# Attention and MLP on one TensorE stream: a slot's attention work at 14 points instead of 7

## The chip, the cores and the metric

The kernel runs on one core of one Trainium2 chip. The metric is the device time of one execution in microseconds (us).

## The reference

The reference is an attention block with normed queries and keys, followed by a two-layer MLP without biases. Inputs are float32; the two MLP weights come as float64.

```python
# q, k, v: (8 batches, 12 heads, 448 positions, 64)
q_n, k_n = (rmsnorm(q, g_q), rmsnorm(k, g_k))     # x / sqrt(mean(x*x) + 1e-6) * g
scores = (1 / 8) * q_n @ k_n.T                    # softmax over keys follows
attn_out = softmax(scores) @ v
x = attn_out.transpose(0, 2, 1, 3).reshape(3584, 768)
h = x @ w_in                                      # 768 x 2048
out = (h - tanh(h)) @ w_out                       # 2048 x 768
```

## The kernel before

The attention of one batch and two heads is a step; there are 8 x 6 = 48 steps, and the work around a step is a slot. The MLP is a Python generator that emits one matmul at a time, batch after batch. A slot emits its attention work by hand and calls `run(ns)` between pieces of it; `run` takes matmuls from the generator until their nominal time has been reached. [...]

**The MLP's stream.** From the second batch on each layer is done by seven products for every set of blocks instead of eight (Strassen's scheme in Winograd's form, order 1, 5, 6, 2, 3, 7, 4). A batch's hidden layer has 4 sets of 7 products of 6 matmuls (168 in all), its output layer 3 sets of 7 products of 8 matmuls (168). Every matmul has 224 columns. `product` (L738) emits the matmuls (L750), then the follow-up that earlier products left in `late["todo"]`, then `use`, which reads the product's PSUM bank. These follow-ups are: copies of product 1 on ACT (L804, L867), sums on DVE (L806 for product 5, L808 for 6, L812 and L813 for 7, L816 for 3, L820 for 4; L869 to L881 in the output layer), tanh on ACT and the subtraction on DVE for product 2 (L786, L787), the same on POOL for the others (L787), the factors of the next layer (L797, L798 on DVE, L799 and L831 on POOL), and the output's transpose (L845 on DVE). Three PSUM banks serve the products. Products 2, 3 and 7 accumulate in the bank of products 1, 5 and 6 and so wait until that has been read. Weights come through a ring of six slots that SP fills five products ahead (L397, L399).

**The slots from the second batch's MLP on** (`slot`, s from 12 to 47). A slot begins with the visit: the scores of step s+1 for the last chunk of keys (L521), then the values of step s mixed with the other scores of step s+1, the exponentials on ACT (L527), and the division (L687 on ACT, L688 and L692 on DVE). Then follow 56 matmuls of the stream, in eight calls of `run` of 7 matmuls each; between them stand pieces of work for later steps. In slot s they are:

- for step s+1: the sum of the exponentials over chunks of keys (`add`, L552 and L553; `add_last`, L560); `fold` turns it on DVE (L657) and reduces it (L659); `gather` copies the parts together on ACT (L667); `spread_sums` reduces, inverts and widens (L675, L676, L678) and turns back (L680).
- for step s+2, from step 15 on by blocks of 32: `square_blocks` (ACT, L466), `norm_blocks` (reduce L473, four copies L475, L476 and L477 on DVE, and the power -1/2 on POOL, L478), `scale_blocks` (DVE, L485), `turn_blocks` for q (DVE transpose L495) and for k (DVE transpose L499, then ACT's multiplication by the gains, L500). Step 14 is still turned by TensorE (`turn`).
- loads on SP: v of step s+2 and q, k of step s+3 (L462) at the head of the stream part; in slot 12 alone the q, k of step 15 stand late in it.

So kT of step s+2, made in slot s, is read by the first matmul of slot s+1. A batch's MLP fills six slots: three hidden slots (s mod 6 = 0, 1, 2), then three output slots. In a hidden slot the products end after these counts of the slot's matmuls: first 6, 12, ... 54; second 4, 10, ... 52; third 2, 8, ... 56. In an output slot they end at 8, 16, ... 56.

Of the kernel before, what the change touches and what calls it, by code (L numbers as in the profile page):

```python
# [9 lines left out]
F32 = mybir.dt.float32  # L10
# [3 lines left out]
ALU = mybir.AluOpType  # L14
# [130 lines left out]
def bounded_path(tc, ctx, q, k, v, moe_w_in, moe_w_out, out, g_col, ident, ones, half_ones, neg_half, early):  # L145
# [17 lines left out]
    nc = tc.nc  # L163
# [17 lines left out]
    BL = 32  # L181
# [33 lines left out]
    def load(s, names):  # L215
        b, hp = steps[s]
        for name in names:
            src = {"q": q, "k": k, "v": v}[name]
            if s == 0 and name != "v":
                t = early[name]  # L220
            else:
                shape = [CP, 2, NCH, D] if name == "q" else [P, NCH, 2, D] if name == "k" else [P, 2, NCH, D]
                t = nat.tile(shape, F32, name=f"{name}_nat", bufs=3 if name == "v" else 2)
                fetch(nc, name, t, src[b, 2 * hp : 2 * hp + 2], in_order(s))
            loaded[name, s] = t
# [176 lines left out]
    normed, turned, probs, sums, whole, xT, tt = {}, {}, {}, {}, {}, {}, {}  # L402

    def squares(s):
        squares_of(nc, early["sq"], early["n"], loaded["q", s], loaded["k", s])

    def norm(s):
        rr = normed[s] = small.tile([P, 2, 2 * NCH], F32, name="rr", bufs=3) if s else early["rr"]
        if s:
            norm_of(nc, rr, early["sq"], early["n"], neg_half)  # L410
# [16 lines left out]
    def turn(s, tk, tq):  # L427

        rr, n = normed.pop(s), early["n"]
        kn = loaded.pop(("k", s))  # L430
        for c in range(NCH):
            nc.tensor.transpose(tk[:, c * P : (c + 1) * P], kn[:, c].rearrange("p h d -> p (h d)"), ident)
        kT = qkp.tile([P, S], F32, name="kT")
        nc.scalar.mul(kT, tk[:, :S], g_col)
        for c in range(NCH):
            nc.tensor.transpose(
                tq[:, c * CP : (c + 1) * CP], n[:, c].rearrange("p h d -> p (h d)"), ident[:CP, :CP]
            )
        qT = qkp.tile([P, S], F32, name="qT")
        nc.scalar.copy(out=qT, in_=tq[:, :S])  # L440
        turned[s] = rr, kT, qT
# [3 lines left out]
    FIRST, NJ = 2, S // BL  # L445
    TURNED = 2 * NP + 3

    def by_blocks(s):
        return has(s) and s >= TURNED
# [14 lines left out]
    def square_blocks(s):  # L464
        sq = normed[s] = late["blocks"].tile([P, 2, NJ, BL], F32, name="qk_n", bufs=1)
        nc.scalar.activation(  # L466
            sq.rearrange("p i j d -> p (i j d)"), loaded["qk", s].rearrange("p i j d -> p (i j d)"), AF.Square
        )

    def norm_blocks(s):  # L470

        mine, other = (late["blocks"].tile([P, 2 * NJ], F32, name=name, bufs=2) for name in ("rr_mine", "rr_other"))
        nc.vector.reduce_sum(mine, normed[s].rearrange("p i j d -> p (i j) d"), axis=AX.X)  # L473
        for g in range(P // BL):
            nc.vector.tensor_copy(out=other[g * BL : (g + 1) * BL], in_=mine[(g ^ 1) * BL : ((g ^ 1) + 1) * BL])  # L475
        nc.vector.tensor_tensor(out=mine, in0=mine, in1=other, op=ALU.add)  # L476
        nc.vector.tensor_scalar(out=mine, in0=mine, scalar1=1.0 / D, scalar2=1e-6, op0=ALU.mult, op1=ALU.add)  # L477
        nc.gpsimd.tensor_tensor(  # L478
            out=mine, in0=mine, in1=neg_half[:, :1].to_broadcast([P, 2 * NJ]), op=ALU.pow
        )  # L480
        normed["rr", s] = mine

    def scale_blocks(s):
        n, rr = normed[s], normed.pop(("rr", s))
        nc.vector.tensor_tensor(  # L485
            out=n.rearrange("p i j d -> p (i j) d"), in0=loaded.pop(("qk", s)).rearrange("p i j d -> p (i j) d"),
            in1=rr[:, :, None].to_broadcast([P, 2 * NJ, BL]), op=ALU.mult,
        )
# [15 lines left out]
    def sc_bank():  # L504
        return bank_of("sc")
# [34 lines left out]
    def full(s):  # L540

        return probs[s, 0][:, :, 0], probs[s, 1][:, :, 1], probs[s, 2][:, :, 0]

    def add(s):

        if s <= NP + NP // 2:
            sums[s] = []
            return
        t = early["sum"]
        sums[s] = [t]  # L550
        p = full(s)
        nc.vector.tensor_tensor(out=t, in0=p[0], in1=p[1], op=ALU.add)  # L552
        nc.vector.tensor_tensor(out=t, in0=t, in1=p[2], op=ALU.add)  # L553

    def add_last(s):
        last = probs[s, KF][:, :, 0]
        for n in range(2 if sums[s] else 0):
            t = sums[s][0]
            part = t[n * KR : (n + 1) * KR, :, n * HS : (n + 1) * HS]
            nc.vector.tensor_tensor(out=part, in0=part, in1=last[n * KR : (n + 1) * KR], op=ALU.add)  # L560
# [90 lines left out]
    FOLDED = 2 * NP + 1  # L651

    def fold(s):

        t = sums.pop(s)[0].rearrange("p h s -> p (h s)")
        turned_sum = late["blocks"].tile([P, 2 * S], F32, name="sum_T")
        nc.vector.transpose(out=turned_sum, in_=t)  # L657
        part = late["blocks"].tile([P, 2 * NJ], F32, name="sum_32")
        nc.vector.reduce_sum(part, turned_sum.rearrange("p (i k) -> p i k", k=BL), axis=AX.X)  # L659
        acc = whole[s] = late["blocks"].tile([2 * BL, P // BL, NJ], F32, name="sum_g")  # L660
        whole["part", s] = part

    def gather(s, h):

        acc, part = whole[s], whole["part", s]
        for g in range(P // BL):
            nc.scalar.copy(  # L667
                out=acc[h * BL : (h + 1) * BL, g], in_=part[g * BL : (g + 1) * BL, h * NJ : (h + 1) * NJ]
            )

    def spread_sums(s):

        acc = whole[s]
        total = late["blocks"].tile([2 * BL, NJ], F32, name="sum_all")
        nc.vector.reduce_sum(total, acc.rearrange("p g j -> p j g"), axis=AX.X)  # L675
        nc.vector.reciprocal(total, total)  # L676
        wide = late["blocks"].tile([2 * BL, NJ, BL], F32, name="sum_w")
        nc.vector.tensor_copy(out=wide, in_=total[:, :, None].to_broadcast([2 * BL, NJ, BL]))  # L678
        rs = whole[s] = late["blocks"].tile([2 * BL, S], F32, name="rs_T")
        nc.vector.transpose(out=rs, in_=wide.rearrange("p j k -> p (j k)"))  # L680

# [33 lines left out]
    late = {}  # L715
# [223 lines left out]
    def run(ns):  # L939

        spent[1] += ns
        while spent[0] + 1.0 < spent[1]:
            took = next(stream, None)
            if took is None:
                return
            spent[0] += took
# [10 lines left out]
    def has(s):  # L957
        return 0 <= s < NS
# [69 lines left out]
    def slot(s):  # L1028

        gap = gap_ns(s)  # L1030
        av = av_banks
        if has(s + 1):
            scores(s + 1, KF)
        if s < FOLDED:
            last_values(s, av)
            totals(s, sc_bank())
            divide(s, values(s, av))
            for c in range(KF):
                scores(s + 1, c)
        else:  # L1040
            visit(s, av)
        if has(s + 2):
            load(s + 2, "v")
        if by_blocks(s + 3) and s + 3 > TURNED:
            load_blocks(s + 3)
        blocks = by_blocks(s + 2)
        run(gap / 2)
        if has(s + 1):
            add(s + 1)
        if blocks:  # L1050
            square_blocks(s + 2)
        run(gap / 2)
        if blocks:
            norm_blocks(s + 2)
        elif has(s + 2):
            turn(s + 2, sc_bank(), sc_bank())
        ahead = has(s + 3) and not by_blocks(s + 3)
        if ahead:
            squares(s + 3)
        if has(s + 4) and not by_blocks(s + 4):  # L1060
            load(s + 4, "qk")
        run(gap / 2)
        folded = has(s + 1) and s + 1 >= FOLDED
        if has(s + 1):
            add_last(s + 1)
        if folded:
            fold(s + 1)
        run(gap / 2)
        if blocks:
            scale_blocks(s + 2)  # L1070
        if ahead:
            norm(s + 3)
        if folded:
            gather(s + 1, 0)
        run(gap / 2)
        if blocks:
            turn_blocks(s + 2, 0)
        if folded:
            gather(s + 1, 1)
        run(gap / 2)  # L1080
        if blocks:
            turn_blocks(s + 2, 1)
        if s + 3 == TURNED:
            load_blocks(s + 3)
        if ahead:
            norm_q(s + 3)
        run(gap / 2)
        if folded:
            spread_sums(s + 1)
        run(gap / 2)  # L1090

    load(0, "qk")
    load(1, "qk")
# [355 lines left out]
```

## Time and profile before

| | |
|---|---|
| median of 3 runs | 1391.6 us (1391.22 to 1391.68) |
| the profiled execution's own time | 1391.42 us |
| its span in the profile | 1389.6 us |
| TensorE busy | 1354.1 us (97% of the span) |
| VectorE (DVE) busy | 941.0 us (68%) |
| ScalarE (ACT) busy | 504.7 us (36%) |
| GpSimd (POOL) busy | 561.8 us (40%) |
| granted TensorE clock | 0.992 |
| L478, the power | 33 times, 4.8 us each |
| DVE's L485 waiting for L478 | 15.4 us in 21 waits |
| PE's L750 waiting for L806 | 4.2 us in 7 waits |

Times in a timeline count from the span's start. A line gives start, duration, engine, code line, operation, output<-input and, in brackets, how long the engine was idle before it and what released it. PE is the matmul, PEld the load of its weights, which can overlap it. SPq and the like are an engine's issuing queue. The ends of matmuls are modelled, so stalls of TensorE are best read from the starts.

### The profile page before, as it was taken

How to read it: one execution, taken by the hardware profiler on the slowest of the kernel's cores; microseconds unless marked ns; L12 is line 12 of the kernel's file. 1: busy time of each engine (PE TensorE's matmuls, PEld its weight loads, DVE VectorE, ACT ScalarE, POOL GpSimd, SP SyncE). 2: the span in 40 equal slices, each digit the busy share in tenths (PEclk: the TensorE clock that was granted, in tenths of full speed). 3: DMA queues.
4: the chain of work that ended last, by engine and by line, in shares of the span. 5: the costliest groups of instructions: out<-in, count | busy, mean ns of one | idle time of the engine just before them, and what ended most of it. 6: DMA issues, size and time to landing. Idle time of an engine off the chain costs nothing.

```text
span 1389.6 us, 29917 instructions
## 1 busy us (share of the span) xinstructions
PE 1354.1 (97%) x11840; PEld 1128.4 (81%) x11840; DVE 941.0 (68%) x1545; ACT 504.7 (36%) x1147; POOL 561.8 (40%) x345
## 2 busy tenths in 40 slices
PE   7989899999999999999999999999999999999997
PEld 3458654478898898899889988988988998899997
DVE  4899888856876788567866668657875677633311
ACT  7856554234322433324332343324333234301100
POOL 4656565223642356225444236323552354402310
PEclk9999999999999999999999999999999999999999
DMA  7888778766666666666657666666567667366663
GB/s 170 187 218 240 249 232 222 206 181 170 177 181 160 177 172 165 176 170 181 178 152 195 177 156 188 172 162 183 165 167 176 181 173 189 100 189 184 191 194 90
DMA packets 367657, 249.91 MB, mean 180 GB/s; under 512 B 281748, under 2 KB 309780, under 8 KB 367508
## 3 DMA queue, kind: packets, MB, share of 16 engines
q1 hardware_dynamic: 367504, 247.90, 66.5%
q8 instruction: 96, 1.57, 0.5%
q14 instruction: 53, 0.43, 0.1%
q10 hardware_dynamic: 4, 0.00, 0.0%
HBM read 214.40 MB, written 33.42 MB: 178 GB/s over the span
## 4 chain that ended last, share of the span: by engine, by line
PE 85%; DMA 6%; DVE 4%; SPq 2%; ACT 1%; issue 1%; POOL 1%; ACTq 0%; DVEq 0%; POOLq 0%
PE mm L750 65%; PE sc L521 8%; PE sc L582 6%; PE mm L915 4%; DMA w_raw<-in_moe_w_in_dram 2%; DMA w_f<-w_out 1%; PE sc L570 1%; DMA gT<-in_moe_w_in_dram 1%; DMA w_raw<-in_moe_w_out_dram 1%; DMA k_nat<-in_k_dram 1%; SPq L272 1%; DVE w_out L82 1%; DVE w_out L79 1%; PE sc L620 1%; DVE w_out L335 0%
## 5 line engine op out<-in xcount | busy, mean ns | idle before, releaser
L750 PE MATMUL mm<-xT,w_f 128*128 128x224 f32 x1392 | 278.5, 354 | 1.7 <-DVE s L806 1.7
L750 PEld LDWEIGHTS mm<-xT,w_f 128*128 128x128 f32 x1392 | 261.3, 190 | 16.0 <-issue 10.2
L750 PEld LDWEIGHTS mm<-gT,w_f 128*128 128x128 f32 x1344 | 252.8, 190 | 12.8 <-issue 12.8
L750 PE MATMUL mm<-gT,w_f 128*128 128x224 f32 x1344 | 263.0, 354 | 0.0
L478 POOL TENSOR_TENSOR rr_mine<-rr_mine,neg_half 128x28 f32<-128x28 f32 x33 | 159.7, 4839 | 218.2 <-DVE rr_mine L477 218.2
L521 PE MATMUL sc<-qT,kT 64*32 64x448 f32 (+1 forms) x3072 | 217.4, 503 | 10.0 <-ACT p_last L527 9.0
L750 PE MATMUL mm<-tt,w_f 128*128 128x224 f32 x1044 | 208.7, 353 | 0.0
L750 PEld LDWEIGHTS mm<-tt,w_f 128*128 128x128 f32 x1044 | 197.0, 190 | 4.4 <-issue 4.4
L787 POOL TENSOR_TENSOR gT<-s,th 128x448 f32<-128x448 f32 x96 | 120.4, 1262 | 197.0 <-ACT th L786 188.2
L750 PE MATMUL mm<-tg,w_f 128*128 128x224 f32 x1008 | 197.5, 352 | 0.0
L750 PEld LDWEIGHTS mm<-tg,w_f 128*128 128x128 f32 x1008 | 190.7, 190 | 0.0
L521 PEld LDWEIGHTS sc<-qT,kT 64*32 64x32 f32 x3072 | 71.1, 107 | 78.5 <-issue 56.2
L688 DVE TENSOR_TENSOR xT<-xT,sc 128x448 f32<-128x448 f32 x35 | 21.7, 621 | 166.5 <-PE sc L521 110.8
L710 POOL TENSOR_TENSOR tt<-xT,tt 128x224 f32<-128x224 f32 x23 | 31.1, 1353 | 234.2 <-DVE xT L692 212.0
L667 ACT COPY sum_g<-sum 32x14 f32<-32x14 f32 x280 | 56.3, 201 | 186.2 <-DVE sum L659 180.5
L582 PE MATMUL sc<-p,v_nat 64*32 64x448 f32 x1120 | 110.5, 536 | 0.0
L786 ACT ACTIVATE th<-s 128x448 f32<-128x448 f32 x96 | 55.2, 575 | 112.7 <-DVE s L812 59.8
L527 ACT ACTIVATE p<-sc 128x448 f32<-128x448 f32 x132 | 71.7, 543 | 51.7 <-PE sc L521 39.1
L915 PE MATMUL mm<-gT,w_out 128*128 128x448 f32 x192 | 75.9, 551 | 0.2 <-POOL w_out L90 0.2
L915 PEld LDWEIGHTS mm<-gT,w_out 128*128 128x128 f32 x192 | 36.3, 193 | 38.3 <-issue 35.8
L582 PEld LDWEIGHTS sc<-p,v_nat 64*32 64x32 f32 x1120 | 40.6, 107 | 31.0 <-issue 31.0
L142 POOL TENSOR_TENSOR rr<-rr,neg_half 112x8 f32<-112x8 f32 (+1 forms) x30 | 49.0, 1660 | 33.7 <-DVE rr L141 33.6
(151 smaller groups left out, 1828.3 us busy)
## 6 DMA issues: line engine op xcount, KB each, us to landing
w_f<-w_in SPq DMA_DIRECT2D x196, 384.0 KB, 3.3
w_f<-w_out SPq DMA_DIRECT2D x147, 512.0 KB, 4.2
w_raw<-in_moe_w_out_dram SPq DMA_DIRECT2D x16, 768.0 KB, 5.2
out_dram<-th SPq DMA_DIRECT2D x192, 56.0 KB, 1.9
w_in<-w_out SPq DMA_DIRECT2D x21, 384.0 KB, 5.9
qk_nat<-in_q_dram SPq DMA_DIRECT2D x132, 56.0 KB, 2.5
qk_nat<-in_k_dram SPq DMA_DIRECT2D x132, 56.0 KB, 2.6
v_nat<-in_v_dram SPq DMA_DIRECT2D x72, 96.0 KB, 3.7
```

The source lines that it names most:

```text
L142: nc.gpsimd.tensor_tensor(out=r, in0=r, in1=neg_half[:rows], op=ALU.pow)
L478: nc.gpsimd.tensor_tensor(out=mine, in0=mine, in1=neg_half[:, :1].to_broadcast([P, 2 * NJ]), op=ALU.pow)
L521: nc.tensor.matmul(tiles[h][i * BL : (i + 1) * BL, :n], lhsT=kT[r, c * P + at : c * P + at + BL], rhs=qT[r, first : first + n], start=True ...
L527: nc.scalar.activation(p[:, h, c if c < 2 else 0, :], tiles[h][:, :n], AF.Exp, scale=1.0 if rr is None else rr[:, 0, 2 * c + h : 2 * c + h ...
L582: nc.tensor.matmul(av[g][i * BL : (i + 1) * BL, :S], lhsT=v_nat[keys, h, c, m * BL : (m + 1) * BL], rhs=p[keys, h], start=first, stop=True ...
L667: nc.scalar.copy(out=acc[h * BL : (h + 1) * BL, g], in_=part[g * BL : (g + 1) * BL, h * NJ : (h + 1) * NJ])
L688: nc.vector.tensor_tensor(out=x, in0=x, in1=av[1][:, :S], op=ALU.add)
L710: eng.tensor_tensor(out=t2, in0=x22, in1=t1, op=ALU.subtract)
L750: nc.tensor.matmul(bank[:, f * HS : (f + 1) * HS], lhsT=w[:, c * width + f, :], rhs=moving[p](c), start=(first and f == 0 and c == 0), sto ...
L786: nc.scalar.activation(th, h, AF.Tanh, bias=0.0, scale=1.0)
L787: eng.tensor_tensor(out=g[:, rows, cols], in0=h, in1=th, op=ALU.subtract)
L915: nc.tensor.matmul(bank[:, :S], lhsT=w_out_row(f, n // HC)[:, n % HC * P : (n % HC + 1) * P], rhs=g[:, f, :], start=(f == 0), stop=(f == C ...
```

## The change

The eight calls of `run` in `slot` become fifteen, each of 56/15 matmuls nominally, and 14 points lie between them. The helpers are cut finer: the third term of the sum, the meeting of the norm's blocks, the power, the fold's reduction and the turn of the spread sums get functions of their own. The order of the points changes as well: the scaling comes after the first gather, and the turn of k is the last point, behind `spread_sums` and the turn of the sums. No instruction is added or removed. In slots from 12 on `ahead` is never true, and neither is the load of q, k by rows.

```diff
+        normed["rr", s] = mine, other
+
+    def meet_blocks(s):
+        mine, other = normed["rr", s]
         for g in range(P // BL):
             nc.vector.tensor_copy(out=other[g * BL : (g + 1) * BL], in_=mine[(g ^ 1) * BL : ((g ^ 1) + 1) * BL])
         nc.vector.tensor_tensor(out=mine, in0=mine, in1=other, op=ALU.add)
         nc.vector.tensor_scalar(out=mine, in0=mine, scalar1=1.0 / D, scalar2=1e-6, op0=ALU.mult, op1=ALU.add)
+        normed["rr", s] = mine
+
+    def power_blocks(s):
+        mine = normed["rr", s]
         nc.gpsimd.tensor_tensor(
...
-    def add(s):
+    def add(s, now=True):
...
-        nc.vector.tensor_tensor(out=t, in0=t, in1=p[2], op=ALU.add)
+        if now:
+            add_third(s)
+
+    def add_third(s):
+        for t in sums[s]:
+            nc.vector.tensor_tensor(out=t, in0=t, in1=full(s)[2], op=ALU.add)
...
         nc.vector.transpose(out=turned_sum, in_=t)
+        whole["turned", s] = turned_sum
+
+    def fold_rest(s):
+        turned_sum = whole.pop(("turned", s))
         part = late["blocks"].tile([P, 2 * NJ], F32, name="sum_32")
         nc.vector.reduce_sum(part, turned_sum.rearrange("p (i k) -> p i k", k=BL), axis=AX.X)
...
+    def turn_sums(s):
+        wide = whole[s]
         rs = whole[s] = late["blocks"].tile([2 * BL, S], F32, name="rs_T")
         nc.vector.transpose(out=rs, in_=wide.rearrange("p j k -> p (j k)"))
...
-        run(gap / 2)
-        if has(s + 1):
-            add(s + 1)
-        if blocks:
-            square_blocks(s + 2)
-        run(gap / 2)
-        if blocks:
-            norm_blocks(s + 2)
...
-        run(gap / 2)
-        if blocks:
-            turn_blocks(s + 2, 1)
-        if s + 3 == TURNED:
-            load_blocks(s + 3)
...
-        run(gap / 2)
-        if folded:
-            spread_sums(s + 1)
-        run(gap / 2)
+        work = (
+            ((following, lambda: add(s + 1, False)), (blocks, lambda: square_blocks(s + 2))),
+            ((following, lambda: add_third(s + 1)),),
+            ((blocks, lambda: norm_blocks(s + 2)), (not blocks, turn_rows)),
+            (
+                (blocks, lambda: meet_blocks(s + 2)), (ahead, lambda: squares(s + 3)),
+                (has(s + 4) and not by_blocks(s + 4), lambda: load(s + 4, "qk")),
+            ),
+            ((following, lambda: add_last(s + 1)), (blocks, lambda: power_blocks(s + 2))),
+            ((folded, lambda: fold(s + 1)),),
+            ((folded, lambda: fold_rest(s + 1)),),
+            ((ahead, lambda: norm(s + 3)), (folded, lambda: gather(s + 1, 0))),
+            ((blocks, lambda: scale_blocks(s + 2)),),
+            ((folded, lambda: gather(s + 1, 1)),),
+            ((blocks, lambda: turn_blocks(s + 2, 0)), (ahead, lambda: norm_q(s + 3))),
+            ((folded, lambda: spread_sums(s + 1)),),
+            ((folded, lambda: turn_sums(s + 1)),),
+            ((blocks, lambda: turn_blocks(s + 2, 1)), (s + 3 == TURNED, lambda: load_blocks(s + 3))),
+        )
+        for point in work:
+            run(4 * gap / (len(work) + 1))
+            for wanted, fn in point:
+                if wanted:
+                    fn()
+        run(4 * gap / (len(work) + 1))
```

More of the change, by code (lines that the diff above doesn't have):

```diff
@@ L480, in norm_blocks @@
         )
-        normed["rr", s] = mine
     def scale_blocks(s):
@@ L676, in spread_sums @@
         nc.vector.reciprocal(total, total)
-        wide = late["blocks"].tile([2 * BL, NJ, BL], F32, name="sum_w")
+        wide = whole[s] = late["blocks"].tile([2 * BL, NJ, BL], F32, name="sum_w")
         nc.vector.tensor_copy(out=wide, in_=total[:, :, None].to_broadcast([2 * BL, NJ, BL]))
+    def turn_sums(s):
+        wide = whole[s]
         rs = whole[s] = late["blocks"].tile([2 * BL, S], F32, name="rs_T")
@@ L1046, in slot @@
         blocks = by_blocks(s + 2)
-        run(gap / 2)
-        if has(s + 1):
-            add(s + 1)
-        if blocks:
-            square_blocks(s + 2)
-        run(gap / 2)
-        if blocks:
-            norm_blocks(s + 2)
-        elif has(s + 2):
-            turn(s + 2, sc_bank(), sc_bank())
-        ahead = has(s + 3) and not by_blocks(s + 3)
[L1058 to L1061, printed above, removed]
-        run(gap / 2)
@@ L1063, in slot @@
-        folded = has(s + 1) and s + 1 >= FOLDED
-        if has(s + 1):
-            add_last(s + 1)
-        if folded:
-            fold(s + 1)
-        run(gap / 2)
-        if blocks:
[L1070 to L1074, printed above, removed]
-        run(gap / 2)
[L1076 to L1081, printed above, removed]
-            turn_blocks(s + 2, 1)
@@ L1083, in slot, with turn_rows @@
-        if s + 3 == TURNED:
-            load_blocks(s + 3)
[L1085 to L1088, printed above, removed]
-            spread_sums(s + 1)
-        run(gap / 2)
+        ahead = has(s + 3) and not by_blocks(s + 3)
+        following = has(s + 1)
+        folded = following and s + 1 >= FOLDED
+        def turn_rows():
+            if has(s + 2):
+                turn(s + 2, sc_bank(), sc_bank())
+        work = (
[17 more added lines that the diff above has]
+        )
```

## Prediction

> **What bounds the kernel now.** I read the page's busy times first, then the table of windows cut at the slots, then the timelines of one slot of each sort. The first line below is the page's, the rest is the table for three neighbouring slots: a window's length, then PE, PEld, DVE, ACT and POOL busy.
>
> ```profile
> PE 1354.1 (97%) x11840; PEld 1128.4 (81%) x11840; DVE 941.0 (68%) x1545; ACT 504.7 (36%) x1147; POOL 561.8 (40%) x345
> ...
> 480.70:507.50 26.80, 26.80 (x248) 23.49 (x240) 20.75 (x34) 10.37 (x26) 11.88 (x6) 1.00 0.61 161
> 507.50:535.10 27.60, 27.30 (x248) 23.31 (x240) 23.40 (x38) 11.10 (x27) 16.12 (x10) 1.00 0.68 179
> 535.10:561.90 26.80, 26.80 (x248) 23.49 (x240) 18.02 (x30) 8.31 (x23) 11.22 (x7) 1.00 0.60 162
> ```
>
> A slot is 56 matmuls of the MLP's stream (21.38 us, 0.382 each) and 5.4 us of attention on TensorE, together 26.80. Five of a batch's six slots last just that; only the third of the hidden layer lasts 27.60. TensorE sets the end, its own work stays as it is, and the change can only take away or add a TensorE stall. The third slot's 0.80 us is explained by the timeline:
>
> ```profile
> 521.43 1.09 DVE L659 TENSOR_REDUCE sum<-sum_T 128x28 f32<-128x896 f32 x1
> 522.43 0.61 DVE L806 TENSOR_TENSOR s<-mm,s 128x448 f32<-128x448 f32 x1
> ...
> 523.02 2.01 DVE L485 TENSOR_TENSOR qk_n<-qk_nat,rr_mine 128x896 f32<-128x896 f32 x1
> 523.10 2.19 PEld L750 LDWEIGHTS mm<-xT,w_f 128*128 128x128 f32 x12 [0.65 <-DVE s L806]
> ```
>
> VectorE has worked without a break since 508.28 and comes late to L806, which frees the PSUM bank that product 3 accumulates in. L806 stands behind the whole fold (L657, L659). L808 then costs the remaining 0.2 to 0.3.
>
> [...] L808, L675 and L680 keep the code's order, and an instruction moved back in the code waits for all that now stands ahead. [...] L485 lasts 1.09 us beside an idle POOL and 2.01 beside a busy one (above). That is my main uncertainty.
>
> **The change part by part.** Nothing is added or removed. Before, the points stand after 7, 14, 21, 28, 35, 42 and 49 matmuls of a slot; after, at multiples of 56/15, which the loop rounds up to 4, 8, 12, 15, 19, 23, 27, 30, 34, 38, 42, 45, 49 and 53. A product's own follow-up stands ahead of a point at the same matmul.
>
> *Costed at nothing.* The square (L466, 0.95 us) goes from 7 to 4; ACT is 36% busy. The adds (L552, L553) are parted by a product's follow-up. The norm's reduce goes from 14 to 12, its copies to 15. The power (L478, 4.8 us) goes from 14 to 19, but no other POOL instruction lies between, so it starts when L477 is done, as before. The scale goes from 28 to 34 (2.3 us later), so its waits of at most 0.9 us for the power (15.4 us in all) vanish; VectorE has spare time in those slots, and TensorE gains nothing. The gathers (four copies, 0.88 us a call) and L675 to L680 have room until the next visit's L692. One-off: the eight loads of load_blocks(15) go on SP from 42 to 53, behind two of the ring's loads; issued from about 311.6 to 315.7 and landing 2.5 us later they are there by 318.2, and their square runs at 320.85. What queues behind, the next slot's v and q/k loads and ring loads, is 2 to 3 us late against five products of 2.3 us in advance. The turn of slot 14 goes from 14 to 12, once.
>
> *The gain.* In the third slot the fold's reduce (1.00 from start to start) moves behind L806, which then starts at about 521.43 and ends at 522.04; product 3 wants the bank at 522.7. The 0.80 goes, six times: 4.8 us.
>
> *The loss.* turn_blocks(s, 1), the transpose L499 and the scaling L500 of kT, goes from 42 to 53. The next slot's first TensorE instruction (L521, keys of the last chunk) reads this kT, three matmuls or 1.1 us later, and all of TensorE queues behind it. L499 to L500's end takes 0.66 + 0.67 from start, and a release reaches PE 0.06 later (L806 ended at 523.04, PEld started at 523.10): 1.39 us. That alone exceeds 1.1 us, and what stands ahead of L499 decides:
>
> ```profile
> 499.81 0.62 DVE L499 STREAM_TRANSPOSE kT<-qk_n 128x448 f32<-128x448 f32 x1
> ...
> 500.47 0.67 ACT L500 ACTIVATE kT<-kT,g_col 128x448 f32<-128x448 f32 x1 [3.61 <-DVE kT L499]
> ...
> 501.39 0.54 ACT L786 ACTIVATE th<-mm 128x448 f32<-128x448 f32 x1 [0.25 <-PE mm L750]
> ...
> 501.81 0.64 DVE L680 STREAM_TRANSPOSE rs_T<-sum_w 64x448 f32<-64x448 f32 x1
> 502.38 0.58 DVE L787 TENSOR_TENSOR gT<-mm,th 128x448 f32<-128x448 f32 x1
> 502.73 0.18 PEld L521 LDWEIGHTS sc<-qT,kT 64*32 64x32 f32 x16 [0.28 <-issue]
> ```
>
> *Second hidden slot (above).* kT is ready at 501.14 and wanted at 502.73. After, L499 stands behind L787 of product 2, which ends at matmul 52. Its tanh cannot start before 501.39; L787 follows its end by 0.07 (the pair at 485.50 and 486.11): 502.00. L499 0.54 later, 502.54; L500 503.20 to 503.87; PE 503.93. Stall 1.2 us. This rests on a PE-gated start and is firm below (1.1); if VectorE is late too, 1.6.
>
> *Third hidden slot.* After L806 at 521.43 the queue is, from start to start: L806 0.59, L659 1.00, L808 0.54, L485 1.93, L787 0.51, L495 0.55, L816 0.51, L675 to L678 0.94, L680 0.57, L812 0.51, L813 0.54. L499 starts at 529.62 and PE gets kT at 531.01; without the old stall it wants it at 529.55. That is 1.5; if L485 meets a free POOL, 0.8 less, and the floor, L812 gated by matmul 50 at 527.44, gives 0.35. I take 1.1, so 0.3 net of the 0.8 gained.
>
> *First hidden slot.* L820 starts at 470.73, gated by matmul 42. Then L820 0.54, L495 0.55, L675 to L678 1.51 (0.94 without POOL), L797 0.69, L798 0.54, L680 0.57, and 1.39 for kT: 476.52 against 475.92, 0.6. Without the POOL collision it is 0.0; if L797 and L798 collide too (1.66 and 1.29 in the neighbouring slot), 2.2. I take 0.6.
>
> *The three output slots.* The last gate is L875 at matmul 48:
>
> ```profile
> 554.25 0.39 DVE L875 TENSOR_TENSOR s<-mm,s 128x224 f32<-128x224 f32 x1 [1.52 <-PE mm L750]
> 554.56 0.38 DVE L876 TENSOR_TENSOR s<-mm,s 128x224 f32<-128x224 f32 x1
> ```
>
> 554.25 + 0.31 + 0.29 + 0.57 (L680) + 1.39 = 556.81, wanted at 557.16: no stall, with 0.35 to spare.
>
> *Sum.* 33 slots make a kT by blocks (13 to 45): five first, six second, six third hidden slots, sixteen output slots. 6 x 1.2 + 6 x 0.3 + 5 x 0.6 + 16 x 0 = 12.0 us. The profiled execution took 1391.42 (span 1389.6), 0.2 below the median of the runs: 1391.42 + 12.0 = 1403.4.
>
> **The rivals.**
> 1. *Faster: kT comes in time and only the 0.8 goes.* The point is the start of L499 in the second hidden slot: up to 502.73 - 1.39 = 501.34 costs nothing. For it: kT has 1.6 us to spare there now, and the third slot's stall is real. Against it: L787 stands ahead and its tanh starts at 501.39. 1391.4 - 4.8 = 1386.6. Chance 9%.
> 2. *Break-even.* The waits cost about the 4.8 that the third slot returns, as when only the second slot stalls, by 0.8, because some follow-up runs earlier than I think. 1391.5. Chance 5%.
> 3. *The output slots stall too.* A POOL collision of 0.8 on their VectorE queue turns 0.35 of room into 0.45 of stall: 16 x 0.45 = 7.2 more, 1410.6. Against it: POOL is idle at their end. Chance 8%.
> 4. *The change doesn't do what it says.* VectorE's order follows the code, so only the sizes can fail.
>
> The forecast itself has 78%.
>
> **How the numbers follow.** About 0.2% (2.8 us) is what a measurement of this kernel tells from no change. Lowest of the likeliest case: 6 x 1.1 - 6 x 0.45 + 0 = 3.9, 1395.3. Highest: 6 x 1.6 + 6 x 0.7 + 5 x 1.6 = 21.8, 1413.2. With rival 3 inside, the range is 1393.5 to 1414.0; rival 1, rival 2 and a tail stay out. Faster 9%, within 5%, slower 86%.
>
> **What would show it.** Right: PE L521 waits for ACT kT L500 in the list of waits, some 17 times, about 1.2 us in the second hidden slots; L806 no longer holds PE in the third; L485 waits no more for L478; output slots at 26.80. Wrong: hidden slots at 26.80 and no wait on L500.

## The result and the profile after

The changed kernel takes 1403.75 us (median of 6 runs, 1402.79 to 1405.29) against 1391.37 for the kernel before in the same comparison. The ratio is 1.0094, with a 95% interval of 1.0081 to 1.0107: slower by 12.4 us. The profiled execution took 1402.79 us, its span is 1401.0.

Line numbers have shifted. In the changed kernel L773 is the MLP's matmul (L750 before), L530 the scores (L521), L508 and L509 the turn and the scaling of kT (L499, L500), L829, L831 and L839 the sums of products 5, 6 and 3 (L806, L808, L816), L835 and L836 those of product 7 (L812, L813), L809 the tanh and L810 its subtraction (L786, L787), L820 and L821 the factors (L797, L798), L494 the scaling by the norm (L485), L567 the second add (L553), L671 and L678 the fold (L657, L659), L488 the power (L478), L697 and L703 the widening copy and the turn of the sums (L678, L680), L711 the division's first instruction on VectorE (L688).

The table of windows of the changed kernel, cut at the first matmul of a slot's stream, shows the four sorts of slot in a row: first, second and third hidden slot, first output slot. The columns are length, then PE, PEld, DVE, ACT and POOL busy.

```profile
455.17:482.58 27.41, 26.89 (x248) 23.53 (x240) 19.84 (x34) 10.65 (x26) 10.86 (x6) 1.00 0.74 191
482.58:511.43 28.85, 26.96 (x249) 23.61 (x241) 21.44 (x34) 10.57 (x26) 11.88 (x6) 1.00 0.59 159
511.43:538.47 27.04, 26.81 (x241) 23.46 (x240) 21.78 (x38) 11.07 (x27) 17.07 (x10) 1.00 0.64 166
538.47:565.29 26.82, 26.82 (x248) 23.49 (x240) 17.80 (x30) 8.32 (x23) 11.22 (x7) 1.00 0.60 162
```

Against an undisturbed slot of 26.8 the first hidden slot is 0.6 too long, the second 2.0, the third 0.2; the output slot is whole. Before, only the third was too long, by 0.8. The list of waits of the changed kernel names who holds TensorE. The columns are total, times and longest; PE's own line and that of its weight loads:

```profile
PE sc L530 <- ACT kT L509: 15.5, 17, 2.0
...
PEld sc L530 <- ACT kT L509: 21.5, 17, 2.3
```

These are 17 waits for kT at a slot's start, and no third hidden slot waits for product 5's sum any more. A weight load at a slot's start idles 0.28 us even when nothing is late (output slots, 557.16 before and 559.86 after), so 21.5 - 17 x 0.28 = 16.7 us are stall. Less 6 x 0.8 = 4.8 us, the old stall that the third slots no longer have, that is 11.9 of the 12.4 us measured.

### The profile page after: what moved, and what is told of

It is laid out like the page before. It is cut to its first block, busy times and chain, and to the rows that moved or that the text cites. A ratio compares the mean times of both kernels' runs of the same rounds, so it can differ in the third digit from the quotient of the medians.

```text
span 1401.0 us, 29899 instructions
## 1 busy us (share of the span) xinstructions
PE 1351.1 (96%) x11840; PEld 1129.0 (81%) x11840; DVE 929.6 (66%) x1545; ACT 507.0 (36%) x1147; POOL 571.1 (41%) x345
## 4 chain that ended last, share of the span: by engine, by line
PE 75%; DVE 14%; POOL 3%; DMA 2%; ACT 2%; issue 2%; SPq 1%; DVEq 0%; ACTq 0%
PE mm L773 54%; PE sc L530 9%; PE sc L596 6%; PE mm L938 4%; POOL rr_mine L488 2%; PE sc L584 1%; DVE qk_n L494 1%; DVE tg L820 1%; ACT kT L509 1%; DVE w_out L335 1%; PE sc L634 1%; DVE kT L508 1%; PE mm L634 1%; DVE sum_w L697 1%; DVE s L831 1%
## 5 line engine op out<-in xcount | busy, mean ns | idle before, releaser
L773 PE MATMUL mm<-xT,w_f 128*128 128x224 f32 x1392 | 275.4, 354 | 0.0
L773 PEld LDWEIGHTS mm<-xT,w_f 128*128 128x128 f32 x1392 | 262.2, 190 | 10.2 <-issue 9.5
L773 PEld LDWEIGHTS mm<-gT,w_f 128*128 128x128 f32 x1344 | 252.8, 190 | 12.8 <-issue 10.6
L773 PE MATMUL mm<-gT,w_f 128*128 128x224 f32 x1344 | 263.0, 354 | 0.0
L488 POOL TENSOR_TENSOR rr_mine<-rr_mine,neg_half 128x28 f32<-128x28 f32 x33 | 159.8, 4841 | 218.3 <-DVE rr_mine L482 218.3
L530 PE MATMUL sc<-qT,kT 64*32 64x448 f32 (+1 forms) x3072 | 218.2, 503 | 26.6 <-ACT kT L509 15.5
L773 PE MATMUL mm<-tt,w_f 128*128 128x224 f32 x1044 | 208.7, 353 | 0.0
L810 POOL TENSOR_TENSOR gT<-s,th 128x448 f32<-128x448 f32 x96 | 121.9, 1276 | 199.7 <-ACT th L809 181.2
L773 PEld LDWEIGHTS mm<-tt,w_f 128*128 128x128 f32 x1044 | 197.0, 190 | 4.4 <-issue 4.4
L773 PE MATMUL mm<-tg,w_f 128*128 128x224 f32 x1008 | 197.5, 352 | 0.0
L773 PEld LDWEIGHTS mm<-tg,w_f 128*128 128x128 f32 x1008 | 190.7, 190 | 0.0
L530 PEld LDWEIGHTS sc<-qT,kT 64*32 64x32 f32 x3072 | 72.3, 107 | 96.5 <-issue 52.1
L711 DVE TENSOR_TENSOR xT<-xT,sc 128x448 f32<-128x448 f32 x35 | 21.8, 622 | 174.7 <-PE sc L530 115.7
L809 ACT ACTIVATE th<-s 128x448 f32<-128x448 f32 x96 | 55.3, 576 | 103.1 <-DVE s L839 42.0
L509 ACT ACTIVATE kT<-kT,g_col 128x448 f32<-128x448 f32 x33 | 22.0, 667 | 140.4 <-DVE kT L508 140.4
```

The lines of the kernel that those rows point to most:

```text
L488: nc.gpsimd.tensor_tensor(out=mine, in0=mine, in1=neg_half[:, :1].to_broadcast([P, 2 * NJ]), op=ALU.pow)
L509: nc.scalar.mul(kT, kT, g_col)
L530: nc.tensor.matmul(tiles[h][i * BL : (i + 1) * BL, :n], lhsT=kT[r, c * P + at : c * P + at + BL], rhs=qT[r, first : first + n], start=True ...
L773: nc.tensor.matmul(bank[:, f * HS : (f + 1) * HS], lhsT=w[:, c * width + f, :], rhs=moving[p](c), start=(first and f == 0 and c == 0), sto ...
L809: nc.scalar.activation(th, h, AF.Tanh, bias=0.0, scale=1.0)
L810: eng.tensor_tensor(out=g[:, rows, cols], in0=h, in1=th, op=ALU.subtract)
```

## The experiments

Every comparison has its own runs of the kernel before, so its time differs a little from one to the next. Ratios are to the kernel before; in the comparisons below they differ by up to 0.0007 from the quotient of the two medians.

**The turn of k back ahead of the sums.** The changed kernel with nothing but the order of the last three points altered:

```diff
-            ((folded, lambda: spread_sums(s + 1)),),
-            ((folded, lambda: turn_sums(s + 1)),),
             ((blocks, lambda: turn_blocks(s + 2, 1)), (s + 3 == TURNED, lambda: load_blocks(s + 3))),
+            ((folded, lambda: spread_sums(s + 1)),),
+            ((folded, lambda: turn_sums(s + 1)),),
```

> The changed kernel with one point moved: the turn of k goes from the last point (53) to the twelfth (45), ahead of spread_sums and turn_sums, which take 49 and 53. Theory A (the whole loss is kT coming late to the next slot's first matmul): the 17 waits on kT vanish, the third hidden slot keeps its gain, so the time is that of the kernel before less 6 x 0.8, about 1386.6 us, and every slot lasts 26.8. Rival B (the finer points cost by themselves, by work that meets badly on VectorE and POOL): the time stays above 1395 us.

Measured: 1383.97 us against 1389.82, ratio 0.9958 (0.9943 to 0.9973). The wait on kT is gone altogether. The longest waits of PE that remain all lie before 240 us, ahead of the second batch's MLP:

```profile
PE sc L530 <- ACT p_last L536: 9.1, 4, 4.8
PE mm L432 <- DVE rr L141: 5.1, 1, 5.1
PE mm L773 <- DVE s L829: 2.5, 1, 2.5
```

Theory A holds: fifteen pieces of the stream cost nothing, the last place of the turn of k costs all. This version is faster than both kernels, and the gain of 0.8 us in six slots (0.35%) lies within its interval.

**The turn of k late, alone.** The kernel before with its seven points:

```diff
         run(gap / 2)
-        if blocks:
-            turn_blocks(s + 2, 1)
         if s + 3 == TURNED:
...
             spread_sums(s + 1)
-        run(gap / 2)
+        run(gap * 2 / 7)
+        if blocks:
+            turn_blocks(s + 2, 1)
+        run(gap * 3 / 14)
```

> The kernel before with its seven points, and only the turn of k taken out of its place at 42 and put at 53, behind spread_sums at 49. Theory A: second hidden slot 1.5 us late (L787 starts at 502.38, kT's 1.9 us follow, wanted at 502.73), third 1.2, first 0.6, and now the output slots too, by 0.6 (555.80 + 0.57 + 1.39 = 557.76 against 557.16): 6 x 1.5 + 6 x 1.2 + 5 x 0.6 + 16 x 0.6 = 29 us, about 1420 us. Rival B: with the seven points kept the loss is small, below 1396 us.

Measured: 1415.42 us against 1389.82, ratio 1.0177 (1.0154 to 1.0200): 25.6 us slower by the medians, 24.6 by the ratio. All 33 slots now wait, so rival B falls:

```profile
PE sc L521 <- ACT kT L500: 22.8, 33, 1.1
```

The stalls are 1.16 in the second hidden slot, 0.65 in the third, about 1.05 in the first and 0.55 in an output slot (idle less 0.28): 6 x 1.16 + 6 x 0.65 + 5 x 1.05 + 16 x 0.55 = 24.9 us. Theory A has the cause, but its single terms miss: 1.5 and 1.2 were too much for the second and third hidden slot, 0.6 too little for the first. An output slot, in the timeline of this kernel:

```profile
562.20 0.64 DVE L680 STREAM_TRANSPOSE rs_T<-sum_w 64x448 f32<-64x448 f32 x1
...
562.77 0.59 DVE L499 STREAM_TRANSPOSE kT<-qk_n 128x448 f32<-128x448 f32 x1
563.39 0.67 ACT L500 ACTIVATE kT<-kT,g_col 128x448 f32<-128x448 f32 x1 [6.96 <-DVE kT L499]
...
564.11 0.18 PEld L521 LDWEIGHTS sc<-qT,kT 64*32 64x32 f32 x16 [0.83 <-ACT kT L500]
```

The spread (0.95 us) stands between product 7's sums and kT here; the changed kernel has it four matmuls earlier, and that is what spares its output slots.

**The fold whole again, and the fold parted alone.** Which part of the change removed the old stall? The forecast said the fold's reduction, moved behind product 5's sum. First it was put back ahead of that sum, in the version with the turn of k at 45:

```diff
-            ((folded, lambda: fold(s + 1)),),
-            ((folded, lambda: fold_rest(s + 1)),),
+            ((folded, lambda: fold(s + 1)), (folded, lambda: fold_rest(s + 1))),
+            (),
```

> The same as the kernel with the turn of k at 45, but the fold is whole again: its reduction stands directly behind its transpose at 23, ahead of product 5's sum. My step (the reduction behind that sum takes the third hidden slot's stall away): the 0.8 us comes back six times, about 5 us more than with the parted fold. Rival C (VectorE is early at that sum for other reasons: in the changed kernel it starts 12.0 us after the slot's first matmul against 14.3 before, and the reduction is only 1.0 of these 2.3): no stall, the time within 1 us of the parted fold's.

Measured: 1384.66 us, ratio 0.9958 (0.9945 to 0.9971), the same as with the parted fold (1383.97). L829 starts 13.0 us after the division's L711 (506.37 to 519.38), later than the 11.9 with the parted fold of the changed kernel (511.48 to 523.39) and still early enough: no third hidden slot waits for it. Rival C holds. Then the parting was done alone on the kernel before (fold at 21, its reduction at 27 by `run(gap * 3 / 7)`, the rest of the points as they were):

> The kernel before with one part of the change alone: the fold's reduction goes from 21 to 27, behind product 5's sum L806. By the forecast's step L806 starts 1.0 us earlier in the third hidden slot (521.4), product 3 no longer waits, and 0.8 us go six times: ratio 0.9966. Theory F (VectorE's backlog only moves on): reduction and scaling now stand ahead of L808, which ends 1.0 + 1.9 + 0.5 us after 522.0, at 525.5, where product 7 wants its bank at about 525.0: most of the stall comes back there, ratio 0.998 to 1.000.

Measured: ratio 0.9999 (0.9990 to 1.0009). In this kernel L811 is product 5's sum and L813 product 6's. VectorE first, then the weight load of product 7:

```profile
521.70 0.58 DVE L811 TENSOR_TENSOR s<-mm,s 128x448 f32<-128x448 f32 x1
522.21 1.06 DVE L664 TENSOR_REDUCE sum<-sum_T 128x28 f32<-128x896 f32 x1
523.40 2.01 DVE L485 TENSOR_TENSOR qk_n<-qk_nat,rr_mine 128x896 f32<-128x896 f32 x1
525.33 0.61 DVE L813 TENSOR_TENSOR s<-mm,s 128x448 f32<-128x448 f32 x1
```

```profile
525.99 2.19 PEld L755 LDWEIGHTS mm<-xT,w_f 128*128 128x128 f32 x12 [0.90 <-DVE s L813]
```

Product 5's sum is in time, and the reduction that moved makes product 6's late: the same stall, one product on. Theory F holds.

**The adds parted alone.** On the kernel before, the first add and the square stand at 4, the second add at 8, behind product 7's sums:

```diff
-        run(gap / 2)
+        run(gap * 2 / 7)
         if has(s + 1):
-            add(s + 1)
+            add(s + 1, False)
         if blocks:
             square_blocks(s + 2)
-        run(gap / 2)
+        run(gap * 2 / 7)
+        if has(s + 1):
+            add_third(s + 1)
+        run(gap * 3 / 7)
```

> The kernel before with another part alone: the second add L553 goes from 7 (directly behind the first) to 8 matmuls, behind product 7's two sums, the first add and the square to 4. Theory G (the third hidden slot's stall came from L553 colliding with POOL's subtraction, 1.83 us instead of 1.09): VectorE gains 0.8 to 0.9 us ahead of L806 and L808, both stalls go, ratio 0.9966, L553 lasts 1.08 us there. Rival: the order alone doesn't shift the collision, ratio 1.000.

Measured: 1384.60 against 1390.80 us, ratio 0.9958 (0.9945 to 0.9972). Theory G holds in the main: this part alone brings all of the gain. In this kernel L558 is the second add and L792 POOL's subtraction. The second add with the subtraction that it meets, before and then with the adds parted:

```profile
511.61 1.24 POOL L787 TENSOR_TENSOR gT<-s,th 128x448 f32<-128x448 f32 x1 [10.70 <-ACT th L786]
...
511.96 1.83 DVE L553 TENSOR_TENSOR rows<-rows,p_full 128x896 f32<-128x896 f32 x1
```

```profile
509.10 1.08 DVE L558 TENSOR_TENSOR rows<-rows,p_full 128x896 f32<-128x896 f32 x1
...
509.40 1.77 POOL L792 TENSOR_TENSOR gT<-s,th 128x448 f32<-128x448 f32 x1 [0.28 <-ACT th L791]
```

Before, POOL starts first and VectorE takes 1.83; this is product 3's subtraction. With the adds parted that one has gone by (it starts at 507.87), and the add meets the next, product 7's. VectorE now starts first and takes 1.08, and POOL takes 1.77, for which VectorE waits nowhere in that slot: it works without a break up to 525.36.

The first add and the square have moved to 4 as well, but they aren't the cause: in both kernels VectorE works without a break from the division on (508.28 before, 504.54 here), and the first add starts 2.50 us after that. From there to product 5's sum VectorE needs 14.15 us before and 13.02 here. Of the 1.13 us, 0.76 are the second add's. The other 0.37 lie in the first add and in product 7's second sum, which are followed sooner (1.00 and 0.53 from start to start instead of 1.18 and 0.72); the instruction that now follows doesn't read their result. Whether the 0.76 alone would have been enough was not tried.

**Half the power.** Why is the second hidden slot 2.0 late and not 1.2? This kernel takes the power over q's columns only and leaves k's sums of squares without it:

```diff
-            out=mine, in0=mine, in1=neg_half[:, :1].to_broadcast([P, 2 * NJ]), op=ALU.pow
+            out=mine[:, :NJ], in0=mine[:, :NJ], in1=neg_half[:, :1].to_broadcast([P, NJ]), op=ALU.pow
```

> The changed kernel with the power taken over q's half of the columns only (k's sums of squares are left without the power), which halves POOL's 4.8 us. Theory D (the second hidden slot is 0.8 us later than forecast because POOL's three subtractions queue behind the power and then collide with VectorE's factors and scaling): the second slot's stall falls from 2.0 to about 1.2 us, the time by 6 x 0.8 to about 1399 us. Rival E (VectorE's own order makes it late there): L494 and the factors keep their place, the time stays within 1.5 us of the changed kernel's.

Measured: 1396.71 us, ratio to before 1.0051 (1.0035 to 1.0066) against the changed kernel's 1.0094. The second slot's stall is 1.44 - 0.28 = 1.16. The tanh, the factors and the subtraction ahead of kT in that slot and the weight load that waits, first in the changed kernel, then with half the power:

```profile
496.18 1.54 DVE L820 TENSOR_TENSOR tg<-gT 128x448 f32<-128x448 f32 x1 [0.43 <-POOL gT L810]
497.83 1.37 DVE L821 TENSOR_TENSOR tg<-gT,tg 128x448 f32<-128x448 f32 x1
499.12 2.02 DVE L494 TENSOR_TENSOR qk_n<-qk_nat,rr_mine 128x896 f32<-128x896 f32 x1
...
502.62 0.55 ACT L809 ACTIVATE th<-mm 128x448 f32<-128x448 f32 x1 [4.54 <-PE mm L773]
...
504.05 0.58 DVE L810 TENSOR_TENSOR gT<-mm,th 128x448 f32<-128x448 f32 x1
504.56 0.62 DVE L508 STREAM_TRANSPOSE kT<-qk_n 128x448 f32<-128x448 f32 x1
...
505.93 0.18 PEld L530 LDWEIGHTS sc<-qT,kT 64*32 64x32 f32 x16 [2.24 <-ACT kT L509]
```

```profile
494.04 0.61 DVE L820 TENSOR_TENSOR tg<-gT 128x448 f32<-128x448 f32 x1
494.76 0.62 DVE L821 TENSOR_TENSOR tg<-gT,tg 128x448 f32<-128x448 f32 x1
495.30 2.02 DVE L494 TENSOR_TENSOR qk_n<-qk_nat,rr_mine 128x896 f32<-128x896 f32 x1
...
501.58 0.62 DVE L810 TENSOR_TENSOR gT<-mm,th 128x448 f32<-128x448 f32 x1 [0.83 <-ACT th L809]
...
503.51 0.18 PEld L530 LDWEIGHTS sc<-qT,kT 64*32 64x32 f32 x16 [1.44 <-ACT kT L509]
```

The power takes 2.58 us (from 488.64) instead of 4.79 (from 490.27). With POOL free earlier the factors take 0.61 and 0.62 instead of 1.54 and 1.37 after a wait of 0.43, and L810 waits for its tanh again. Theory D holds, though for the factors and the wait alone: the scaling still takes 2.02. The tanh is the gate (what sets the earliest start) that the forecast counted on, and gives its 1.2.

**Scaling ahead of the first gather.** The changed kernel with the points at 30 and 34 exchanged.

> The changed kernel with the scaling and the first gather exchanged (scaling at 30, gather at 34), so that VectorE scales ahead of the factors in the second hidden slot and fills its wait of 0.4 us for POOL. Theory D (collisions with POOL's three subtractions): scaling and the first factors still collide, only the wait goes, the stall falls from 2.0 to about 1.6 us, the time by 2.4 to about 1401 us. Rival E (the order is the cause): the stall falls to the 1.2 us that the tanh sets, the time by 4.8.

Measured: 1399.88 us, ratio 1.0066 (1.0050 to 1.0082). In the second hidden slots the weight load idles 1.58 us (504.87) to 1.7 at most, so the stall is 1.3 to 1.4, between the two expectations. The factors still collide (1.55 and 1.37), but the wait of 0.43 is filled, and the scaling, which now starts early, takes 1.43 instead of 2.02. So order and collision both count, and they are not independent: the order decides which VectorE instruction meets POOL.

**The power back behind its input.** The changed kernel with `power_blocks` at 15 instead of 19.

> The changed kernel with the power directly behind its input's last step again (15 instead of 19). Forecast's step: POOL has no other instruction between the two places and the power starts when L482 is done, so nothing changes: the changed kernel's time within 1.5 us, stalls on kT of 2.0, 0.3 and 0.6 us as in the changed kernel. Rival: the placing delays or frees the power by a part of four matmuls (up to 1.5 us), and the second hidden slot's stall moves by as much.

Measured: 1403.18 us, ratio 1.0092 (1.0076 to 1.0107), with 17 waits for kT of 15.5 us in all, as in the changed kernel. The power's place costs and brings nothing.

## Why the prediction was right, and where it was not

The mechanism of the loss, the count and the sum were right: 17 stalls on kT, output slots untouched, 1403.4 forecast against 1403.75. The old stall ended as forecast, but not for the reason given. That the sum is so close is luck: two of its terms are wrong by the same amount in opposite directions. VectorE's order followed the code, as forecast: in the traces of both kernels its 1545 instructions start in the order in which the code emits them, and in the second hidden slot L508 starts at 504.56, 0.51 us after the L810 that now stands ahead of it.

The end of the third hidden slot in the changed kernel, to be set against the forecast's queue there:

```profile
529.81 0.64 DVE L703 STREAM_TRANSPOSE rs_T<-sum_w 64x448 f32<-64x448 f32 x1
530.59 0.62 DVE L835 TENSOR_TENSOR s<-mm,s 128x448 f32<-128x448 f32 x1
531.13 0.61 DVE L836 TENSOR_TENSOR s<-mm,s 128x448 f32<-128x448 f32 x1
531.66 0.64 DVE L508 STREAM_TRANSPOSE kT<-qk_n 128x448 f32<-128x448 f32 x1
```

- **First hidden slot: right.** 0.6 forecast, 0.87 - 0.28 = 0.59 measured, the collision of the widening copy with POOL included (L697 takes 1.09 us at 472.97, 0.38 in the second hidden slot at 502.65).
- **Second hidden slot: mis-sized.** 1.2 forecast, 2.0 measured. The step that failed is that the tanh of L787 (L810 now) is the gate. The scaling's move to 34 had been costed at nothing, but there it stands behind the factors of product 1's follow-up, and these wait for POOL's subtractions, which queue behind the power (L488 from 490.27 for 4.79 us, then three L810 from 495.02 for 3.70). L810 starts at 504.05 although its tanh ended at 503.17. The forecast's upper end of 1.6 was too low. Half the power restored the 1.2; the scaling at 30 took 0.6 to 0.7 us away.
- **Third hidden slot: mis-sized the other way.** 1.1 forecast, 0.3 measured. I carried the old backlog on to the slot's end: product 5's sum was to start 13.3 us after the slot's first matmul (508.16 to 521.43). It starts after 12.0: the forecast had counted the reduction's move alone, and lists the parting of the adds, worth 1.1 us here, under "costed at nothing". So VectorE caught up, and only the gate at matmul 50 was left, the floor of 0.35 that I had named: in the lines above L703 ends at 530.45, and L835 starts 0.14 us later. Six times 0.8 too little and six times 0.8 too much make nothing.
- **The gain: right in size, wrong in cause.** The step "the reduction moves behind L806, so the 0.8 goes" failed: with the reduction back the gain stays, and the reduction alone gives none. What brings it is the parting of the adds: product 7's sums now separate the second from the first, so that it meets POOL as the earlier and not the later of the two, which is 0.76 of the 1.13 us that VectorE gains. The changed kernel's L829 starts 12.0 us after the slot's first matmul, against 14.3 before; 1.1 us of this come without the reduction's move, as the version with the whole fold shows (13.0 from the division to L829, against 14.15 before).
- **Output slots: right.** kT was forecast 0.35 ahead of need; in the timeline L509 ends at 559.41 and its reader starts undelayed at 559.86, after the usual 0.28 us.
- **The waits for the power: wrong, at no cost.** I wrote that they vanish; L494 still waits 15.1 us in 15 waits (15.4 in 21 before). Those of the first hidden slots did vanish, and those left lie in output slots. In the output slot of the table above VectorE has nothing between the fold's reduction and the scaling, so the scaling's later place in the code doesn't hold it back: VectorE is ready for it at 550.83, and the power ends at 551.82. TensorE waited for none of it.
- **SP, the square, the gathers: rightly costed at nothing.** The list of PE's waits in the changed kernel names no DMA, no square and no gather.

## What to carry to other kernels

A point in an interleaved stream fixes an order, not a time: ask of each moved piece what gated instruction now stands ahead of it on its engine, and who reads its result first. A producer whose reader is the first instruction of the next stage belongs ahead of work that has a stage's time to spare; here that order alone turned 0.9% slower into 0.4% faster. And when a backlog is the cause, moving one piece behind the late instruction may only make the next one late (the fold parted alone: ratio 0.9999); look for what lengthens the backlog. The order on one engine also decides which of its instructions meets which of another engine, and which of the two starts first: the same add took 1.83 us behind POOL's subtraction and 1.08 ahead of it.

## What the runs showed of the hardware that I had not expected

In these collisions of VectorE and POOL the order of starting went with who pays: the pair of add and subtraction lasts 1.83 and 1.24 us when POOL is first (511.61 before), 1.08 and 1.77 when VectorE is (509.10 with the adds parted); where the other engine is idle they take 1.09 and 1.13 (485.10 and 1321.36 before). I had used the collision only as a spread of durations and not as something that an order can turn round.

Not every POOL instruction lengthened VectorE's. The forecast reckons with a busy POOL in general, but beside the power (L478, 517.89 to 522.98 before) L798 takes 0.63 us and the two instructions of L560 together 1.26, as they do beside an idle POOL (0.62 at 472.52, 1.26 at 1216.03). These runs show the collision beside the subtractions, not beside the power; why is open.

In these traces VectorE also spent less from start to start where the next instruction doesn't read the last one's result: 1.15 us from the fold's transpose to its own reduction (520.28 to 521.43 before), 1.02 to an independent sum (522.37 to 523.39 after); and the two cases named under the parted adds, 1.18 against 1.00 and 0.72 against 0.53. The runs don't isolate this.
